# Sparse attention into a routed expert layer: wider token rows, later gathers, an earlier first pair

## The chip, the cores and the metric

The kernel runs on one core of one Trainium2 chip. The metric is device time of one execution in microseconds; lower is better. Matmuls run on TensorE (PE), elementwise work and reductions on VectorE (DVE), copies out of PSUM and exponentials on ScalarE (ACT). GpSimd (POOL) does small copies and issues most DMAs, among them all indirect ones; SyncE (SP) issues the rest.

## The reference

Attention over 4 images x 8 heads of 768 tokens and 64 columns: each query sees the keys nearer than 16 places and, for each block of 32 tokens, one summary (the columnwise maximum of the keys, the mean of the values). The result, 3072 tokens of 512 columns, goes through a layer of 8 experts of which one is used for each token:

```python
k_sum = k.reshape(B, H, nb, block, D).max(axis=3)      # block = 32
v_sum = v.reshape(B, H, nb, block, D).mean(axis=3)
mask_l = np.abs(pos[:, None] - pos[None, :]) < window  # window = 16
a = softmax over [masked q.k/8, q.k_sum/8 + log(block)]
x = a @ concat(v, v_sum)                               # as (3072, 512) rows
logits = x @ w_gate + modality_bias[modality_id]
e_idx = argmax(logits); gate_w = softmax(logits)[e_idx]
out[token] = gate_w * (relu(x @ w1[e_idx]) @ w2[e_idx])
```

The inputs are drawn once; w1 is 8 x 512 x 1024 and w2 8 x 1024 x 512, all in fp32. The kernel computes in fp16 with fp32 sums.

## The kernel before

The work comes in 16 **pairs** of heads (4 images x 4 pairs), numbered `n`. For each pair, `load` has GpSimd fetch keys, values and queries with a cast to fp16 (three DMAs). `keys` transposes keys and values on TensorE (`pk`), ScalarE copies them into `kv`, and GpSimd copies the borders between chunks of 64 tokens. `summaries` reduces the blocks on VectorE (`ks`), and GpSimd spreads them into `kv` (L236). `queries` transposes the queries, `blocks` the values with their summaries. `scores` (in two halves) multiplies, takes the exponential and a band mask, and `values` (two halves) multiplies with the values and writes the normalized rows into `xb`, a tile of one image's token rows. `features` transposes `xb` into `xT`. Each engine runs its instructions in the order in which the program emits them, and that order is written out by hand: the main loop at the end works on pair `n` while it prepares pairs `n+1` and `n+2` and loads `n+5`.

When an image is done, `route(b)` runs. It is a generator that the main loop advances by `tick()` between other work: a `yield` more is one place later in the order, on every engine. It computes the gate's logits (`pl`), the winning expert (`oh`), the rank of each token among those of its expert with matmuls by triangular and all-ones matrices (`pr`), and counts (`pc`). Then GpSimd writes each token's row of `xb` to its place in `xs`, a DRAM buffer sorted by expert, with six indirect DMAs (L381). A row holds 512 fp16 columns, the gate weight and the token's number. `take` (called by `route`) then makes a list of tiles of 256 rows: whole tiles of one expert for the first three images (2, 4 and 2 tiles), all that is left for the last.

`rows` fetches a tile's rows into `xr`. For the first three images one plain DMA from SyncE does, at a row number read from the list. For the last image the list has a row number for each of 256 places (`gi`), and GpSimd gathers with two indirect DMAs (L458). `weights` loads an expert's weights where they differ from those in the buffer. `expert_tile` is a generator too, advanced by `pump()`: `turn` transposes the rows (`px`, copied to `xg`), the first layer (`ph`, L498) is copied with a relu to `hT`, and the second layer (`pmo`, L509) is scaled by ScalarE into `ot` (L514) and written to the output with two indirect DMAs (L515). The transposes of tile `i+1` lie inside tile `i`. `enlist` takes up a list: it calls `rows` for every tile of it, queues them in `todo`, and `ahead` starts as many as there are weight buffers (two).

13 tiles of 256 rows run in this draw: 0 to 7 from the first three images, beside the attention of later pairs; 8 to 12 after the last one. How many of the last are needed is read by every engine into a register (`nt`, L642) before they run, and a ladder of branches follows.

The lines that matter most:

```python
XW = DM + 4                                    # fp16 columns in a row of xs, xb, xr
...
for j in range(lst["T"]):                      # enlist
    rows(lst, j, lst["i0"] + j)
    todo.append((lst, j, lst["i0"] + j))
ahead()
...
early_constants()                              # before the main loop
keys(0)
load(2)
summaries(0)
queries(0)
scores(0, 0)
```

Of the kernel before, what the change touches and what calls it, by code (L numbers as in the profile page):

```python
# [22 lines left out]
def kernel(  # L23
# [12 lines left out]
    nc = tc.nc  # L36
# [10 lines left out]
    P8 = S // C8  # L47
    WK, NB = 96, S // 32
    KR = WK + NB
    XW = DM + 4  # L50
    RP = N + 256
    NROW = 256 + E * RP
    NWB = 2
# [23 lines left out]
    def load(n):  # L77
        b, cc = pairs[n]
        loaded[n] = []
        for name, src in (("kn", k), ("vn", v), ("qn", q)):  # L80
# [5 lines left out]
            loaded[n].append(dst)  # L86


    load(0)
    load(1)  # L90
    pidx = const.tile([128, 1], FP32, name="pidx")
    nc.gpsimd.iota(pidx, pattern=[[0, 1]], base=0, channel_multiplier=1,
                   allow_small_or_imprecise_dtypes=True)
    cidx = const.tile([128, 128], FP32, name="cidx")
    nc.gpsimd.iota(cidx, pattern=[[1, 128]], base=0, channel_multiplier=0,
                   allow_small_or_imprecise_dtypes=True)
    ident = const.tile([128, 128], FP16, name="ident")
    nc.vector.tensor_scalar(ident, cidx, pidx, None, op0=ALU.is_equal)
    for kv, vb in zip(kvs, vbs):
        nc.vector.memset(kv[:, :, 0, 64:80], 0.0)  # L100
        nc.vector.memset(kv[:, :, NT - 1, 80:96], 0.0)
        nc.vector.memset(kv[:, :, :, KR:128], 0.0)
        nc.vector.memset(vb[0:WK, :, :, D:D + 1], 1.0)
        nc.vector.memset(vb[WK:KR, :, :, D:D + 1], 32.0)
    tok = const.tile([128, NJ], I32, name="tok")
    nc.gpsimd.iota(tok, pattern=[[128, NJ]], base=0, channel_multiplier=1)
    midc = const.tile([NJ, 128], mybir.dt.int64, name="midc")
    nc.sync.dma_start(midc, moe_modality_id.rearrange("(j p) -> j p", p=128))
    mb0 = const.tile([128, 2, E], FP32, name="mb0")
    nc.sync.dma_start(mb0, moe_modality_bias.unsqueeze(0).to_broadcast([128, 2, E]))  # L110
    ge = const.tile([128, 4], FP32, name="ge")
    for i, at in enumerate((32.0, 64.0, 80.0)):
        nc.vector.tensor_scalar(ge[:, i:i + 1], pidx, at, None, op0=ALU.is_ge)
# [57 lines left out]
    def later_constants():  # L171
        for t in xrs[-2:]:
            nc.vector.memset(t, 0.0)
        nc.sync.dma_start(xs[0:256].rearrange("(a p) d -> p a d", p=128), xrs[-1].bitcast(I32))
        yield
        nc.gpsimd.dma_start(wg, moe_w_gate.rearrange("(c p) e -> p c e", p=128))
        nc.vector.tensor_scalar(upper, cidx, pidx, None, op0=ALU.is_gt)
        nc.vector.tensor_copy(prow[:, 0:1], pidx)
        nc.vector.tensor_scalar_add(prow[:, 1:2], pidx, 128.0)
        yield  # L180
        nc.vector.tensor_scalar_mul(k256, cidx[:, 0:KM].unsqueeze(2).to_broadcast([128, KM, E]), 256.0)
        nc.vector.tensor_tensor(rowc, k256, erow[:, None, :].to_broadcast([128, KM, E]), op=ALU.add)
        nc.vector.tensor_copy(tab[:, 2], cidx[:, None, 0:E].to_broadcast([128, KM, E]))
        mdiff = work.tile([128, E], FP32, tag="mdiff", bufs=1, name="mdiff")
        nc.vector.tensor_tensor(mdiff, mb0[:, 1, :], mb0[:, 0, :], op=ALU.subtract)
        yield
        mh = work.tile([NJ, 128], FP16, tag="mh", bufs=1, name="mh")
        nc.vector.tensor_copy(mh, midc.bitcast(I32)[:, 0::2])
        yield
        yield  # L190
        pm = bank([128, NJ], FP16, "pm")
        nc.tensor.transpose(pm, mh, ident[0:NJ, 0:NJ])
        yield
        midf = work.tile([128, NJ], FP32, tag="midf", bufs=1, name="midf")
        nc.vector.tensor_copy(midf, pm)
        yield
        nc.vector.tensor_tensor(base, midf.unsqueeze(2).to_broadcast([128, NJ, E]),
                                mdiff[:, None, :].to_broadcast([128, NJ, E]), op=ALU.mult)
        yield
        nc.vector.tensor_tensor(base, base, mb0[:, 0:1, :].to_broadcast([128, NJ, E]), op=ALU.add)  # L200
# [77 lines left out]
    xbs = {}  # L278

    def values(n, half):  # L280
        b, cc = pairs[n]
        s = st[n]
        pT, vb = s.pop(("pT", half)), s["vb"]
        po = bank([128, 2, 3, D + 1], FP32, "po")
        for h in range(2):
            for tl in range(6):
                nc.tensor.matmul(po[64 * (tl % 2):64 * (tl % 2) + 64, h, tl // 2, :],  # L287
                                 pT[0:KR, h, tl, :], vb[0:KR, 6 * half + tl, h, :])
        rec = work.tile([128, 2, 3], FP32, tag="rec", name="rec")
        nc.vector.reciprocal(rec, po[:, :, :, D])  # L290
        if b not in xbs:
            xbs[b] = work.tile([128, NC, XW], FP16, tag="xb", bufs=2, name="xb")
            nc.vector.tensor_copy(xbs[b][:, :, DM:XW].bitcast(I32)[:, :, 1:2],
                                  tok[:, ds(NC * b, NC)].unsqueeze(2))
        xo = xbs[b][:, 3 * half:3 * half + 3, ts(cc, 128)].rearrange("p c (h d) -> p h c d", h=2)
        nc.vector.tensor_tensor(xo, po[:, :, :, 0:D], rec.unsqueeze(3).to_broadcast([128, 2, 3, D]),  # L296
                                op=ALU.mult)
# [26 lines left out]
    def route(b):  # L324
# [23 lines left out]
        ex = small([128, NC, E], tag="ex")  # L348
        nc.scalar.activation(ex, lg, AF.Exp)
        yield  # L350

        pr = bank([128, NC, E], FP32, "pr")
        nc.tensor.matmul(pr, ident, bc(erow, NC), start=True, stop=False, skip_group_check=True)
# [11 lines left out]
        with nc.allow_low_precision(reason="whole numbers: rows, and counts up to 24"):  # L365
            posi = small([128, NC], U32, tag="posi", bufs=2)
            nc.vector.reduce_sum(posi, rk, axis=AX.X)
            xb = xbs.pop(b)
            nc.vector.reciprocal(xb[:, :, DM:DM + 2].bitcast(FP32), se.unsqueeze(2))
            yield  # L370
            if b == 0:
                nc.vector.reduce_sum(tot, oh.rearrange("p c e -> p e c"), axis=AX.X)
            else:
                t2 = small([128, E], FP16, tag="t2")
                nc.vector.reduce_sum(t2, oh.rearrange("p c e -> p e c"), axis=AX.X)
                nc.vector.tensor_tensor(tot, tot, t2, op=ALU.add)
        yield
        pc = bank([128, E], FP32, "pc")
        nc.tensor.matmul(pc, ones, tot)
# [107 lines left out]
    def expert_tile(i):  # L487
# [6 lines left out]
        for f2 in range(NF // 2):  # L494
            ph = bank([128, 2, 256], FP32, "ph")
            for f in range(2):
                for c in range(NCD):
                    nc.tensor.matmul(ph[:, f, :], w1[:, c, ts(2 * f2 + f, 128)], xg[:, c, :],  # L498
                                     start=(c == 0), stop=(c == NCD - 1))
            yield  # L500
            nc.scalar.activation(hT[:, 2 * f2:2 * f2 + 2, :], ph, AF.Relu)  # L501
        if i + 1 in prep and i + 1 not in heads:
            turn(i + 1)
        for s2 in range(2):
# [22 lines left out]
    def enlist(lst):  # L527
        heads.add(lst["i0"])
        for j in range(lst["T"]):
            rows(lst, j, lst["i0"] + j)  # L530
            todo.append((lst, j, lst["i0"] + j))
        ahead()

    def ahead():

        while todo and todo[0][2] < min(ended[0] + NWB, guessed[0]):
            lst, j, i = todo.popleft()
            weights(lst, j, i)
            pending.append(expert_tile(i))

# [10 lines left out]
    def drain(g):  # L551
        for _ in g:
            pass
# [12 lines left out]
    def weights_ahead(n):  # L566

        for p in {1: (0,), 2: (1, 2), 3: (3,), 4: (4,), 5: (5,), 6: (6,), 7: (7,)}.get(n, ()):
# [5 lines left out]
            if p == 7:  # L574
                guessed[0] = NTILE + NWB
                ahead()

    early_constants()
    keys(0)
    load(2)  # L580
    summaries(0)
    queries(0)
    scores(0, 0)
    blocks(0)
    keys(1)
    load(3)
    summaries(1)
    load(4)
    queries(1)
    side.append(later_constants())  # L590
    for n in range(np_):
        b, cc = pairs[n]
        u = [int(c) for c in UNITS.get(n, "000000")]
        scores(n, 1)
        tick()
        if n and cc == 0:
            features(n - 1)
            assert not side
            side.append(route(b - 1))
        pump(u[0])  # L600
        if n + 2 < np_:
            keys(n + 2)
        if n + 5 < np_:
            load(n + 5)
        weights_ahead(n)
        tick()
        pump(u[1])
        values(n, 0)
        tick()
        if n + 2 < np_:  # L610
            summaries(n + 2)
        tick()
        pump(u[2])
        if n + 2 < np_:
            queries(n + 2)
        tick()
        pump(u[3])
        if n + 1 < np_:
            blocks(n + 1)
            tick()  # L620
            scores(n + 1, 0)
        tick()
        pump(u[4])
        if cc:
            features(n - 1)
        tick()
        values(n, 1)
        tick()
        if b and cc == 1:
            tick(99)  # L630
            enlist(lists[b - 1])
        pump(u[5])
# [6 lines left out]
    r = lists[B - 1]  # L639
    i0 = r["i0"]  # L640
    enlist(r)
    nt = nc.values_load(r["li"][0:1, NSURE + 1, 0:1], min_val=NSURE, max_val=FIN)  # L642
    while todo or len(pending) > 1:
        drain(pending.popleft())
        ended[0] += 1
        ahead()
# [38 lines left out]
```

The softmax here doesn't subtract the row's maximum and nothing guards it: scores larger than these inputs give would overflow.

## Time and profile before

| | |
|---|---|
| time, median of 3 | 269.67 us (268.44 to 271.12) |
| span of the profiled execution | 266.6 us |
| TensorE matmul busy | 193.5 us (73%) |
| VectorE busy | 128.1 us (48%) |
| ScalarE busy | 122.4 us (46%) |
| GpSimd busy | 126.3 us (47%) |
| DMA moved | 27.08 MB |

A share of the span is a mean over stages with different limits: the first pair (to about 15 us), pairs alone (to 77 us), pairs with tiles beside them (to 186 us), and the last image's routing and tiles (from there on). The last output write is issued at 256.25 us; its landing and the ladder of branches close the span. What limits a stage has to be read from its own windows and timeline. In a timeline row the columns are the start and duration in us, the engine (PEld is TensorE's weight load), the line, the operation, output and inputs, shapes and count, and in brackets the engine's idle time before it with what ended that.

### The profile page before, as it was taken

The page shows a single profiled execution, that of the slowest core. Times are in us where ns is not written, and L with a number is a line of the kernel's source. Part 1 is how long each engine was busy: PE and PEld are TensorE (multiplying, and loading weights), DVE is VectorE, ACT ScalarE, POOL GpSimd, SP SyncE. Part 2 cuts the span into 40 slices and gives each one's busy share as a digit, 9 for nine tenths or more (in the row PEclk, how much of TensorE's full clock was granted, in tenths as well). Part 3 has the DMA queues.
Part 4 walks back from the last instruction along what each step waited for, and adds up shares of the span by engine and source line. Part 5 has one row for each costly group of instructions (what it writes and reads, how often), then busy time and mean ns, then how long its engine had stood idle before and what let it go on. Part 6 is the DMA issues. An engine that isn't in the chain of part 4 may idle for free. (4 is left out here: it accounts for less than half of the span.)

```text
span 266.6 us, 6691 instructions
## 1 busy us (share of the span) xinstructions
PE 193.5 (73%) x2684; PEld 137.1 (51%) x2684; DVE 128.1 (48%) x361; ACT 122.4 (46%) x211; POOL 126.3 (47%) x198
## 2 busy tenths in 40 slices
PE   0375966753859895597998776998973829999920
PEld 0264844642747663264767534675751603677610
DVE  0859899661975565096456824753770100111000
ACT  1355894422736572173866435562423113454520
POOL 7529797536661347556132174131576751223220
PEclk9999996555558999577999995999999965999995
DMA  6838999993795948268511022421123321122100
GB/s 84 128 61 117 193 165 200 205 200 109 110 225 84 113 64 183 102 87 182 151 39 42 2 81 83 119 82 40 72 94 122 104 88 39 43 79 80 73 19 0
DMA packets 20090, 27.08 MB, mean 102 GB/s; under 512 B 2876, under 2 KB 16468, under 8 KB 20052
## 3 DMA queue, kind: packets, MB, share of 16 engines
q0 software_dynamic: 17424, 24.17, 45.0%
q1 hardware_dynamic: 2628, 2.41, 3.3%
q8 instruction: 23, 0.38, 0.6%
q14 instruction: 15, 0.12, 0.1%
HBM read 85.27 MB, written 10.25 MB: 358 GB/s over the span
## 5 line engine op out<-in xcount | busy, mean ns | idle before, releaser
L509 PE MATMUL pmo<-w2b,hT 128*128 128x512 f16 x208 | 53.4, 407 | 6.1 <-issue 4.2
L498 PE MATMUL ph<-xg,w1b 128*128 128x256 f16 x416 | 54.7, 283 | 3.6 <-issue 3.6
L515 POOL DMA_INDIRECT out_dram<-ot,at x26 | 25.9, 995 | 49.3 <-ACT ot L514 40.7
L498 PEld LDWEIGHTS <-w1b 128*128 128x128 f16 x416 | 39.6, 100 | 12.4 <-issue 4.8
L272 ACT ACTIVATE pT<-pss 128x384 f16<-128x384 f32 x64 | 28.0, 496 | 29.6 <-PE pss L268 29.3
L501 ACT ACTIVATE hT<-ph 128x512 f16<-128x512 f32 x52 | 30.6, 605 | 20.3 <-remote 13.9
L223 ACT COPY kv<-pk 128x768 f16<-128x768 f16 x32 | 24.5, 814 | 32.8 <-PE pk L222 13.5
L509 PEld LDWEIGHTS <-hT 128*128 128x128 f16 x208 | 20.2, 102 | 30.7 <-issue 8.5
L381 POOL DMA_INDIRECT xs<-xb,posi x24 | 24.5, 1022 | 15.8 <-DVE rec L290 8.4
L514 ACT ACTIVATE ot<-pmo,xr 128x512 f32<-128x512 f32 x26 | 18.0, 692 | 28.9 <-PE pmo L509 26.2
L481 DVE COPY xg<-px 128x1024 f16<-128x1024 f16 x13 | 8.9, 684 | 45.0 <-PE px L479 32.9
L273 DVE TENSOR_TENSOR pT<-pT,bmask 96x768 f16<-96x768 f16 x32 | 19.6, 613 | 17.1 <-ACT pT L272 16.2
L226 POOL COPY kv<-kv 128x352 f16<-128x352 f16 x16 | 8.1, 509 | 28.6 <-ACT kv L223 28.4
L290 DVE RECIPROCAL rec<-po 128x6 f32<-128x6 f32 x32 | 6.0, 187 | 30.6 <-PE pq L244 13.2
L255 PE MATMUL pv<-ident,kv 128*128 128x128 f16 x192 | 18.8, 268 | 1.8 <-POOL kv L236 1.0
L287 PE MATMUL po<-vb,pT 120*64 120x65 f16 x384 | 15.3, 215 | 6.5 <-issue 2.9
L244 PE MATMUL pq<-ident,qn 96*64 96x96 f16 x256 | 13.5, 244 | 7.2 <-issue 6.3
L255 PEld LDWEIGHTS <-kv 128*128 128x128 f16 x192 | 15.8, 123 | 5.2 <-issue 2.2
L296 DVE TENSOR_TENSOR xb<-po,rec 128x384 f16<-128x384 f32 x32 | 17.8, 557 | 1.2 <-issue 0.2
L268 PE MATMUL pss<-qT,kv 64*128 64x64 f16 x384 | 13.3, 211 | 5.9 <-POOL kv L236 5.9
L246 ACT COPY qT<-pq 128x768 f16<-128x768 f16 x16 | 13.0, 810 | 9.6 <-PE pq L244 9.5
L256 ACT COPY vb<-pv 120x768 f16<-120x768 f16 x16 | 12.9, 804 | 8.1 <-PE pv L255 8.1
(122 smaller groups left out, 279.6 us busy)
## 6 DMA issues: line engine op xcount, KB each, us to landing
w1b<-in_moe_w_dram POOLq DMA_DIRECT2D x13, 1024.0 KB
w2b<-in_moe_w_dram POOLq DMA_DIRECT2D x13, 1024.0 KB
kn<-in_k_dram POOLq DMA_DIRECT2D x16, 192.0 KB
vn<-in_v_dram POOLq DMA_DIRECT2D x16, 192.0 KB
qn<-in_q_dram POOLq DMA_DIRECT2D x16, 192.0 KB
xr<-xs SPq DMA_DIRECT2D x8, 258.0 KB, 4.0
w1b<-in_moe_w_dram POOLq DMA_DIRECT2D x4, 512.0 KB
w2b<-in_moe_w_dram POOLq DMA_DIRECT2D x4, 512.0 KB
```

What stands on the lines that cost most here:

```text
L223: nc.scalar.copy(kv[:, i, :, 0:64].rearrange("p t (s c) -> p t s c", c=C8), bass.AP(pk.tensor, pk.offset, [pk.ap[0], [8, NT], [1, 8], [P8, ...
L255: nc.tensor.transpose(pv[:, tl, :], kv[:, 1, 6 * half + tl, :], ident)
L272: nc.scalar.activation(pT[:, h], pss[h], AF.Exp, scale=SCALE)
L273: nc.vector.tensor_tensor(pT[0:WK], pT[0:WK], bmask[0:WK, None, 6 * half:6 * half + 6, :].to_broadcast([WK, 2, 6, 64]), op=ALU.mult)
L287: nc.tensor.matmul(po[64 * (tl % 2):64 * (tl % 2) + 64, h, tl // 2, :], pT[0:KR, h, tl, :], vb[0:KR, 6 * half + tl, h, :])
L296: nc.vector.tensor_tensor(xo, po[:, :, :, 0:D], rec.unsqueeze(3).to_broadcast([128, 2, 3, D]), op=ALU.mult)
L381: apart("xs", nc.gpsimd.indirect_dma_start(out=xs[:, :], out_offset=bass.IndirectOffsetOnAxis(ap=posi[:, c:c + 1], axis=0), in_=xb[:, c, : ...
L498: nc.tensor.matmul(ph[:, f, :], w1[:, c, ts(2 * f2 + f, 128)], xg[:, c, :], start=(c == 0), stop=(c == NCD - 1))
L501: nc.scalar.activation(hT[:, 2 * f2:2 * f2 + 2, :], ph, AF.Relu)
L509: nc.tensor.matmul(po, hT[:, f, ts(s2, 128)], w2[:, f, :], start=(f == 0), stop=(f == NF - 1))
L514: nc.scalar.activation(ot, po, AF.Copy, scale=gt)
L515: apart("out", nc.gpsimd.indirect_dma_start(out=out[:, :], out_offset=bass.IndirectOffsetOnAxis(ap=at[:, s2:s2 + 1], axis=0), in_=ot[:], i ...
```

## The change

It has four parts.

- The rows of `xs`, `xb` and `xr` grow from 516 to 544 fp16 columns, that is from 1032 to 1088 bytes, which is 17 x 64. The added columns of `xb` are set to zero. The aim is that each row begins and ends on a boundary of 64 bytes.
- Of the last image's tiles, `enlist` gathers the rows of the first two only; a new function `fetch` gathers a later tile's rows within the tile two before it (or when the tile is started). The aim is that GpSimd, which issues in order, isn't occupied by ten gathers at once. The register load for the branches moves from ahead of these tiles to between them.
- At the start, two index vectors are made ahead of the first loads; the borders of each pair's buffers are set just before that pair instead of all at once, and the early constants come after the first pair's summaries, so that the first scores can start earlier.
- `route` yields three times more (twice ahead of `pr`, once ahead of `pc`), `later_constants` once more, and at the end of an image `keys(n + 2)` goes ahead of `features` and the new route, so that TensorE has other work while VectorE prepares what a routing matmul needs.

The diff, cut to its core:

```diff
-    XW = DM + 4
+    XW = DM + 32
...
-    load(0)
-    load(1)
     pidx = ...iota;  cidx = ...iota
+    load(0)
+    load(1)
     ident = ...
-    for kv, vb in zip(kvs, vbs):
+    def borders(i):
+        kv, vb = kvs[i], vbs[i]
         nc.vector.memset(kv[:, :, 0, 64:80], 0.0)      # and four more
+    borders(0)
...
     # values
             xbs[b] = work.tile([128, NC, XW], FP16, tag="xb", bufs=2, name="xb")
+            nc.vector.memset(xbs[b][:, :, DM:XW], 0.0)
...
     # route
         nc.scalar.activation(ex, lg, AF.Exp)
+        yield
+        yield
         yield
         pr = bank([128, NC, E], FP32, "pr")
...
+        yield
         yield
         pc = bank([128, E], FP32, "pc")
...
     # expert_tile, after the first layer
+        fetch(i + 2)
         if i + 1 in prep and i + 1 not in heads:
...
     # enlist
-            rows(lst, j, lst["i0"] + j)
+            if lst["gi"] is None or j < 2:
+                rows(lst, j, lst["i0"] + j)
...
+    def fetch(i):
+        for lst, j, i2 in todo:
+            if i2 == i and i not in prep:
+                rows(lst, j, i)
...
     # ahead
-            lst, j, i = todo.popleft()
+            lst, j, i = todo[0]
+            fetch(i)
+            todo.popleft()
...
     # before the main loop
-    early_constants()
     keys(0)
-    load(2)
     summaries(0)
+    load(2)
+    borders(1)
+    early_constants()
     queries(0)
...
     # main loop
         scores(n, 1)
         tick()
+        pump(u[0])
+        if n + 2 < np_:
+            keys(n + 2)
         if n and cc == 0:
             features(n - 1)
             side.append(route(b - 1))
-        pump(u[0])
-        if n + 2 < np_:
-            keys(n + 2)
...
     # the last tiles
-    nt = nc.values_load(r["li"][0:1, NSURE + 1, 0:1], ...)
     while todo or len(pending) > 1:
+        if ended[0] == i0 + NSURE - 2:
+            nt = nc.values_load(r["li"][0:1, NSURE + 1, 0:1], ...)
         drain(pending.popleft())
```

More of the change, by code (lines that the diff above doesn't have):

```diff
@@ L107 @@
     midc = const.tile([NJ, 128], mybir.dt.int64, name="midc")
-    nc.sync.dma_start(midc, moe_modality_id.rearrange("(j p) -> j p", p=128))
     mb0 = const.tile([128, 2, E], FP32, name="mb0")
     nc.sync.dma_start(mb0, moe_modality_bias.unsqueeze(0).to_broadcast([128, 2, E]))
+    nc.sync.dma_start(midc, moe_modality_id.rearrange("(j p) -> j p", p=128))
     ge = const.tile([128, 4], FP32, name="ge")
@@ L376, in route @@
                 nc.vector.tensor_tensor(tot, tot, t2, op=ALU.add)
+        yield
         yield
@@ L576, in weights_ahead @@
                 ahead()
+    keys(0)
+    summaries(0)
+    load(2)
+    borders(1)
     early_constants()
-    keys(0)
-    load(2)
-    summaries(0)
     queries(0)
@@ L585 @@
     keys(1)
+    summaries(1)
     load(3)
-    summaries(1)
     load(4)
+    borders(2)
     queries(1)
@@ L641 @@
     enlist(r)
-    nt = nc.values_load(r["li"][0:1, NSURE + 1, 0:1], min_val=NSURE, max_val=FIN)
     while todo or len(pending) > 1:
+        if ended[0] == i0 + NSURE - 2:
+            nt = nc.values_load(r["li"][0:1, NSURE + 1, 0:1], min_val=NSURE, max_val=FIN)
         drain(pending.popleft())
```

## The prediction

> **What bounds the kernel now.** I read the table by windows of 10 us first, then the timeline of three stretches in which it looked weak, then the list of waits. Of the windows (columns: PE, weight load, DVE, ACT, POOL busy, granted clock, DMA share, GB/s) these carry the argument:
>
> ```profile
> 0.00:10.00 10.00, 2.34 (x48) 2.09 (x48) 3.30 (x24) 3.58 (x4) 5.95 (x15) 1.00 0.81 117
> 10.00:20.00 10.00, 4.97 (x102) 4.49 (x104) 6.59 (x24) 3.82 (x7) 3.69 (x7) 1.00 0.43 65
> 30.00:40.00 10.00, 7.34 (x214) 6.19 (x212) 9.89 (x20) 9.42 (x17) 9.35 (x15) 1.00 1.12 167
> ...
> 200.00:210.00 10.00, 5.68 (x38) 2.87 (x37) 0.76 (x2) 2.77 (x5) 6.85 (x9) 1.00 0.38 116
> 210.00:220.00 10.00, 4.10 (x31) 2.55 (x28) 0.19 (x1) 1.25 (x3) 6.09 (x8) 0.77 0.29 92
> 220.00:230.00 10.00, 9.82 (x55) 5.67 (x56) 0.57 (x2) 4.67 (x9) 2.05 (x4) 0.72 0.14 52
> 230.00:240.00 10.00, 10.00 (x70) 6.33 (x68) 1.52 (x4) 4.66 (x8) 2.05 (x4) 1.00 0.15 55
> ```
>
> There is no single bound. In the first 15 us everything waits for the first pair. From 20 to 190 us several engines share the load (DVE 9.9 of 10 us at 30 to 40). At 230 to 250 TensorE is full: the ideal end. At 200 to 220 nothing is full: TensorE has half its work, VectorE none, and only GpSimd is occupied. The timeline of the start shows why the first scores are late:
>
> ```profile
> 6.35 0.85 PE L222 MATMUL pk<-ident,kn 96*64 96x96 f16 x16 [6.35 <-DVE ident L98]
> ...
> 12.43 0.95 DVE L233 TENSOR_REDUCE ks<-kv 128x24 f16<-128x768 f16 x1
> 13.29 0.94 DVE L235 TENSOR_REDUCE ks<-kv 128x24 f16<-128x768 f16 x1
> 14.30 0.67 POOL L236 COPY kv<-ks 128x576 f16<-128x576 f16 x1 [1.97 <-DVE ks L235]
> 15.03 0.50 PE L268 MATMUL pss<-qT,kv 64*128 64x64 f16 x12 [5.92 <-POOL kv L236]
> ```
>
> The keys were copied by 8.74 us, but VectorE had 3 sets of border memsets, the mask and the early constants ahead of `ks`. In the routing of the first image TensorE stands in order behind VectorE twice:
>
> ```profile
> 54.16 0.20 PE L354 MATMUL pr<-oh,upper 128*128 128x48 f16 x1 [2.57 <-DVE oh L347]
> ...
> 57.38 0.17 PE L379 MATMUL pc<-tot,ones 128*128 128x8 f16 x1 [2.00 <-DVE tot L372]
> ```
>
> And the timeline of the tail:
>
> ```profile
> 202.11 1.07 POOL L458 DMA_INDIRECT xr<-xs,gi  x1 [1.44 <-issue]
> ...
> 208.52 3.67 PE L498 MATMUL ph<-xg,w1b 128*128 128x256 f16 x32
> ...
> 215.19 0.60 ACT L501 ACTIVATE hT<-ph 128x512 f16<-128x512 f32 x1 [5.01 <-remote]
> 215.32 1.02 POOL L515 DMA_INDIRECT out_dram<-ot,at  x1 [0.30 <-DMA xr<-xs,gi]
> ...
> 219.81 0.69 DVE L481 COPY xg<-px 128x1024 f16<-128x1024 f16 x1 [12.09 <-remote]
> ...
> 225.91 3.66 PE L498 MATMUL ph<-xg,w1b 128*128 128x256 f16 x32
> ```
>
> Tile 8 (the first of the last image) starts its first layer at 208.52, tile 9 only at 225.91: 17.4 us. The next tiles start 7.39 us apart (233.31, 240.70, 248.09), so 10.0 us are lost here. The ten gathers run from 202.11 to 215.01, and the consumers of tile 8's matmuls (ACT `hT`, DVE `xg`) stay idle until 215 and 219.5, although the matmuls are recorded by 212.2. TensorE is also recorded in small bursts of about five, with gaps put down to "issue", during the six row writes at 57.5 to 65.1, 104.1 to 111.5 and 153 to 161. So something in long rows of indirect DMAs holds TensorE's completions up; the trace doesn't tell what.
>
> **What the Trainium skill says.** "TensorE: Matmul & The Clock Gate", Part 1: the clock falls to half after an idle window and needs a few us of work to return. The trace agrees: granted clock 0.77 and 0.72 at 210 to 230, and 128x512 matmuls then run 0.42 us apart against 0.21; idle TensorE costs twice. "DMA: Bandwidth & Descriptors", Anatomy of one DMA: about 2 us of an HBM write are the wait for its receipt, beyond issue. The trace has 3.2 us: the last row write is issued by 198.10, and the gathers' wait ends at 201.3. The same page, How a descriptor splits into AXI transactions: a start that isn't on 256 B costs extra beats. Rows of 1032 B start badly, rows of 1088 B start on 64 B and still mostly not on 256; four rows took 0.18 us in the trace, and two 2048 B output rows 0.17. I see no DMA engine that is the limit there, and credit the padding by itself with nothing.
>
> **The change part by part.**
>
> *Start.* The two iotas (0.41 us by their starts, 5.58 to about 5.97) now go ahead of the loads, so every load is 0.4 us later: K lands at 5.8, V's transposes end 0.4 later, and the copies of both at 9.15. `ident` no longer gates (the 6.35 wait goes). VectorE has only one set of borders and the mask before `ks` (work of about 4.5 us from about 2.5, so done by 7). V's reduction, 0.94 after 9.15, ends at 10.1; the POOL copy 0.67 ends near 10.9; first scores at about 11.0 against 15.03: 4.0 us earlier. Against it, `load(2)` moves behind that copy, from 10.39 to 10.9, and its last data land near 16.3 instead of 15.8 (DMA ceased at 15.8 by the packets' times), where pair 2's queries would be wanted at 20.97-4.0=17.0, its keys at 15.3: a wait of up to 0.5. `early_constants` (10.79 to 12.5 before) moves behind `ks`, beside ACT's first exponentials. Credit 3.5; bounds 1.5 and 4.5. It lasts, as loads are issued pairs ahead and TensorE never waits for them after 8.3 us.
>
> *Routing with more yields; `keys` ahead of `features`.* TensorE's waits for `pr` and `pc` are 2.57+2.00 in the first image, 1.08 in the second, 1.29+0.45 in the third: 7.4 us. Its waits of `pt` for `xb` (2.39, 0.89, 0.80: 4.1 us) now lie behind the 32 key transposes. To pay: `pl` now follows `pt` with no other TensorE work between, and needs the `xT` copy (0.55 plus some 0.3 of hand-over), 3 x 0.9=2.7. And the lists come three ticks later; a pair of about 9 us has eight ticks, so some 3 us. Queued behind a list are SP's load of `xr` and, behind that, the `px` transposes; that wait was already 3.06 us at 77.8. In the last image one more `ph` group (1.03) precedes `pr`, so the row writes start about 1.1 us later. I credit a net 1.5 for the three images (bounds -4 and +6) and charge 1.1 in the tail.
>
> *Gathers one tile ahead.* At the head of the last list 4 gathers are issued instead of 10: at 1.31 us apart they end at 202.11+4x1.31=207.4 (plus the 1.1), and tile 8's first layer meets none of the other six. Each later tile gets two (2.6 us) beside its two output writes (2x0.98): 4.6 of 7.39 us of POOL, so they fit, and a gather is asked for a whole tile (7.4 us) before its transposes, against some 4.3 from issue to use at 202.11 to 206.36. Behind a gather on POOL now stand the output writes of that tile, each late by at most 2.6 us, and `ot` has three buffers. Of the 10.0 us lost I keep 2.6 for one pair of gathers during tile 8: gain 7.4. The price of a gather to TensorE is not in the trace by itself; bounds: 0 gained if two gathers hold a tile up as ten did, 10 if not at all.
>
> *Register load of `nt` moved* (L642; TensorE idle 1.36 ahead of 197.88, ACT 5.18): credited with nothing, because tile 8 waits for its rows until 206 anyway; it now falls between full tiles, 0.5 us per queue, behind TensorE's queued matmuls.
>
> *Small ones.* Four memsets of `xb`'s tail (about 0.15 each on VectorE), wider `xr` (5% of 2 x 0.49 us), 5% more row bytes: the row writes are issued at 1.29 us each, so bytes hide behind issue. Nothing. The swap of `mb0` and `midc` frees `g1` earlier, hidden.
>
> Sum: -3.5-1.5-(7.4-1.1)=-11.3, so 269.7-11.3=258.4 us.
>
> **Rivals.**
> *A, as worked out:* 258.4. For it: the 10 us gap stands alone in the tail, and the start is a plain chain. Chance 0.58.
> *B, absorbed:* the front's gain meets full DMA queues (share 1.12 to 1.18 at 30 to 60 us) or the later lists, and the held-up TensorE returns with each pair of gathers; only some 4 us stay: 265.7. For it: VectorE is full at 30 to 40, and the clock may fall in the wait before tile 8. Chance 0.20.
> *C, the aligned rows also end the hold-ups:* three trains of row writes take TensorE some 7 to 10 us for work of 3 to 5, so 4 each: 258.4-12=246.4. Against it: the hold-up at 103.4 begins before the first row write lands, behind output writes whose rows are aligned. Chance 0.12.
> *D, slower:* the lists' 3 us are paid in each of three images (+9 less 4 of saved waits), gathers hold up each of four tiles by 2.6 (so no gain of the 10), the last routing +1.1, the start -3.5: about 272.5. For it: `px` already waits 3.06 on `xr`. Chance 0.10.
>
> **How the numbers follow.** The predicted time is A's. Low 247.5 takes in most of C and the upper bounds of A's parts; high 267.5 takes in B. Out of it are D and part of C, under 2 in 10. Faster by over 1% (under 267.0): A, C and 0.13 of B: 0.83. Within 1%: the rest of B and a little of D: 0.08. Slower: 0.09.
>
> **What would show it.** First scores near 11 us; no TensorE wait at `pr` or `pc` over 1 us; the `px` wait on `xr` in the first image no more than 5 us; after the last row writes four gathers in a row, then pairs; tiles 8 and 9 under 11 us apart, tiles 9 to 12 still 7.4. Wrong if tiles 9 to 12 stretch above 8.5 us, if first scores stay after 13 us, or if TensorE isn't held up any more during the row writes (then C).

## The result, and the profile after

The changed kernel is faster: 249.83 us (249.01 to 250.73, 4 runs) against 269.06 us for the kernel before in the same series (265.48 to 271.12, 4 runs), a ratio of 0.936 with a 95% interval of 0.926 to 0.946. Repeated in two later series the ratio was 0.931 (0.924 to 0.938) and 0.982 (0.970 to 0.994). That the two differ so much is the main finding below. Medians take in all runs, but ratios leave out those in a slower, disturbed state, so a difference given "by the ratio" can be smaller than that of two medians: here it is 17 us, not 19.

The same windows as before the change, now of the kernel after (PE, weight load, DVE, ACT, POOL busy, granted clock, DMA share, GB/s):

```profile
0.00:10.00 10.00, 2.55 (x48) 1.99 (x48) 5.34 (x26) 3.31 (x4) 6.14 (x16) 1.00 0.80 112
10.00:20.00 10.00, 7.08 (x168) 6.29 (x168) 8.16 (x36) 8.61 (x15) 7.09 (x13) 1.00 0.75 105
30.00:40.00 10.00, 7.70 (x187) 6.41 (x183) 9.20 (x18) 8.07 (x15) 8.67 (x15) 0.77 1.19 203
190.00:200.00 10.00, 4.62 (x20) 2.15 (x21) 1.47 (x4) 1.29 (x2) 6.55 (x9) 0.66 0.41 136
200.00:210.00 10.00, 10.00 (x82) 7.48 (x80) 0.76 (x2) 5.65 (x9) 5.20 (x7) 1.00 0.24 80
210.00:220.00 10.00, 10.00 (x80) 6.96 (x78) 1.52 (x4) 4.96 (x8) 4.69 (x9) 1.00 0.30 106
220.00:230.00 10.00, 10.00 (x72) 6.52 (x71) 0.76 (x2) 4.63 (x8) 4.77 (x7) 1.00 0.16 58
```

The second window holds 168 matmuls where it held 102: the pairs begin sooner. One weak window is left before the last tiles (190 to 200), where there were two, and a third at 0.72 of the clock; from 200 on TensorE is full at full clock, with GpSimd's gathers beside it (POOL is busy for 5.2 and 4.7 us of each 10, where the last windows of before had 2.05).

The timeline of the start, in which every step is the one the prediction followed:

```profile
5.15 0.85 PE L227 MATMUL pk<-ident,kn 96*64 96x96 f16 x16 [5.15 <-DMA kn<-in_k_dram]
...
6.88 0.95 DVE L238 TENSOR_REDUCE ks<-kv 128x24 f16<-128x768 f16 x1 [2.20 <-ACT kv L228]
...
8.50 0.95 DVE L240 TENSOR_REDUCE ks<-kv 128x24 f16<-128x768 f16 x1 [0.67 <-ACT kv L228]
...
9.51 0.67 POOL L241 COPY kv<-ks 128x576 f16<-128x576 f16 x1
...
10.42 0.50 PE L273 MATMUL pss<-qT,kv 64*128 64x64 f16 x12 [0.89 <-ACT qT L251]
```

Now the keys' transposes wait for the keys, and the reductions for ScalarE's copies: a chain with no foreign work in it. The routing of the first image, TensorE's rows:

```profile
48.31 0.20 PE L362 MATMUL pr<-oh,upper 128*128 128x48 f16 x1 [1.85 <-DVE oh L353]
...
51.30 0.19 PE L388 MATMUL pc<-tot,ones 128*128 128x8 f16 x1
```

The wait at `pr` fell from 2.57 to 1.85, that at `pc` from 2.00 to nothing. And the tail:

```profile
191.98 1.07 POOL L467 DMA_INDIRECT xr<-xs,gi  x1 [0.30 <-issue]
...
196.00 1.01 POOL L467 DMA_INDIRECT xr<-xs,gi  x1 [0.30 <-issue]
...
199.88 3.66 PE L507 MATMUL ph<-xg,w1b 128*128 128x256 f16 x32
...
203.93 1.05 POOL L467 DMA_INDIRECT xr<-xs,gi  x1 [0.87 <-issue]
...
207.28 0.93 PE L507 MATMUL ph<-xg,w1b 128*128 128x256 f16 x7
```

Four gathers, then a pair in each tile; tile 9 follows tile 8 after 7.40 us instead of 17.39.

So the 18.4 us between the profiled spans (266.6 and 248.2) come in three portions, read off the starts of the same instruction in both: 4.6 by the first scores, 10.0 by the last image's logits (`pl`, 186.15 and 176.19), and 18.6 by tile 9's first layer (225.91 and 207.28). The start gave 4.6, pairs and routing 5.4, the tail 8.7.

One more view matters: the list of waits that the profile puts down to "remote", where an engine waited although the matmul it needed was recorded as ended, and no instruction is named as the releaser. (The ends of matmuls are modelled by the profile, not measured.) All are engines waiting for TensorE. The time given is the engine's whole idle time before the instruction, ordinary waiting included: of the 12.1 us of `xg` below only the last 4.4, from 215.4 to 219.8, lie behind the recorded end of the transposes. First the kernel before, then the kernel after (total us, times, longest):

```profile
ACT hT L501 <- remote: 13.9, 3, 5.2
...
DVE xg L481 <- remote: 12.1, 1, 12.1
...
DVE rec L290 <- remote: 8.6, 1, 8.6
...
ACT kv L223 <- remote: 6.4, 2, 4.2
```

```profile
ACT pT L277 <- remote: 10.7, 3, 5.3
...
DVE rec L295 <- remote: 5.7, 1, 5.7
...
DVE xT L314 <- remote: 4.8, 1, 4.8
...
ACT kv L228 <- remote: 2.6, 1, 2.6
...
ACT qT L251 <- remote: 1.6, 1, 1.6
...
ACT hT L510 <- remote: 0.9, 1, 0.9
```

These are the hold-ups of the prediction. They stand beside trains of indirect DMAs in both kernels. Those of the last tiles (`hT`, `xg`, 26.0 us) are all but gone. Those beside row writes are still there: of the second and third image in the kernel before, of all three in the kernel after.

### The profile page after: what moved, and what is told of

Same layout as the page of the kernel before. It is cut to its first block, busy times and chain, and to the rows that moved or that the text cites. A ratio compares the mean times of both kernels' runs of the same rounds, so it can differ in the third digit from the quotient of the medians.

```text
span 248.2 us, 6696 instructions
## 1 busy us (share of the span) xinstructions
PE 188.5 (76%) x2684; PEld 135.6 (55%) x2684; DVE 125.6 (51%) x365; ACT 122.3 (49%) x211; POOL 125.8 (51%) x198
## 3 DMA queue, kind: packets, MB, share of 16 engines
HBM read 85.46 MB, written 10.44 MB: 386 GB/s over the span
## 5 line engine op out<-in xcount | busy, mean ns | idle before, releaser
L507 PE MATMUL ph<-xg,w1b 128*128 128x256 f16 x416 | 53.1, 278 | 2.7 <-issue 2.5
L519 PE MATMUL pmo<-w2b,hT 128*128 128x512 f16 x208 | 52.8, 401 | 2.9 <-ACT hT L510 1.7
L507 PEld LDWEIGHTS <-w1b 128*128 128x128 f16 x416 | 39.1, 99 | 11.0 <-issue 4.2
L524 ACT ACTIVATE ot<-pmo,xr 128x512 f32<-128x512 f32 x26 | 18.0, 691 | 31.3 <-PE pmo L519 18.5
L390 POOL DMA_INDIRECT xs<-xb,posi x24 | 25.4, 1057 | 8.1 <-issue 5.8
L278 DVE TENSOR_TENSOR pT<-pT,bmask 96x768 f16<-96x768 f16 x32 | 18.2, 570 | 13.8 <-ACT pT L277 13.4
L260 PE MATMUL pv<-ident,kv 128*128 128x128 f16 x192 | 17.5, 257 | 4.4 <-issue 2.5
L260 PEld LDWEIGHTS <-kv 128*128 128x128 f16 x192 | 14.8, 117 | 6.7 <-issue 3.2
L488 PE MATMUL px<-ident,xr 128*128 128x128 f16 x104 | 9.8, 247 | 10.8 <-DMA xr<-xs 6.2
L292 PE MATMUL po<-vb,pT 120*64 120x65 f16 x384 | 14.8, 215 | 3.5 <-issue 2.9
L238 DVE TENSOR_REDUCE ks<-kv 128x24 f16<-128x768 f16 x16 | 15.1, 944 | 3.3 <-ACT kv L228 3.3
```

Of the source, the lines that this page charges most:

```text
L238: nc.vector.reduce_max(ks[:, 0], kv[:, 0, :, 0:64].rearrange("p t (g s) -> p t g s", g=2), axis=AX.X)
L260: nc.tensor.transpose(pv[:, tl, :], kv[:, 1, 6 * half + tl, :], ident)
L278: nc.vector.tensor_tensor(pT[0:WK], pT[0:WK], bmask[0:WK, None, 6 * half:6 * half + 6, :].to_broadcast([WK, 2, 6, 64]), op=ALU.mult)
L390: apart("xs", nc.gpsimd.indirect_dma_start(out=xs[:, :], out_offset=bass.IndirectOffsetOnAxis(ap=posi[:, c:c + 1], axis=0), in_=xb[:, c, : ...
L519: nc.tensor.matmul(po, hT[:, f, ts(s2, 128)], w2[:, f, :], start=(f == 0), stop=(f == NF - 1))
L524: nc.scalar.activation(ot, po, AF.Copy, scale=gt)
```

## The experiments

Twelve kernels ran, in four series on four chips; those of one series shared a chip and runs of the kernel before. The chip of the first pair of profiles is not on record, and no chip served in two series, so a difference between chips cannot be told from one between times. "A chip with hold-ups" below means a series in which they were seen. This table has the landmarks of all profiles, one for each kernel: us from the start of the span to the first scores, and to the first layer of tiles 7, 8 and 9. "Remote" says whether the list of waits has any such line.

| kernel | remote | first scores | tile 7 | tile 8 | tile 9 | 7 to 9 | span |
|---|---|---|---|---|---|---|---|
| before | yes | 15.03 | 194.61 | 208.52 | 225.91 | 31.3 | 266.6 |
| after | yes | 10.42 | 184.41 | 199.88 | 207.28 | 22.9 | 248.2 |
| a_gather10 | no | 10.90 | 174.37 | 190.20 | 197.59 | 23.2 | 238.2 |
| a_narrow | no | 11.01 | 173.57 | 189.13 | 196.53 | 23.0 | 237.2 |
| a_oldstart | no | 15.04 | 175.59 | 191.25 | 198.64 | 23.1 | 239.3 |
| a_oldroute | no | 10.65 | 171.51 | 186.56 | 194.87 | 23.4 | 235.5 |
| a_again | yes | 10.44 | 183.38 | 198.98 | 206.38 | 23.0 | 247.1 |
| b_again | yes | 15.01 | 190.72 | 214.24 | 224.53 | 33.8 | 265.3 |
| a_oldkeys | yes | 10.79 | 185.24 | 200.79 | 208.18 | 22.9 | 248.9 |
| a_oldyield | yes | 10.54 | 182.59 | 197.69 | 205.08 | 22.5 | 245.4 |
| a_third | no | 10.81 | 172.21 | 188.04 | 195.43 | 23.2 | 236.4 |
| a_gather10_2 | no | 10.77 | 173.36 | 188.99 | 196.39 | 23.0 | 236.9 |
| a_lasthead | no | 10.17 | 173.83 | 186.63 | 196.82 | 23.0 | 237.7 |
| b_tail | yes | 15.01 | 190.36 | 205.73 | 213.12 | 22.8 | 253.8 |

**First series: the change with one part undone.** The kernel before took 242.72 us here (55 runs, 239.91 to 249.66), not 269. Nothing in this series can therefore be set against the 249.83 of the changed kernel; the four are compared with each other and with 242.72.

*All ten gathers at the head of the list again:*

```diff
-            if lst["gi"] is None or j < 2:
-                rows(lst, j, lst["i0"] + j)
+            rows(lst, j, lst["i0"] + j)
```

> The changed kernel with all ten gathers of the last image at the head of its list again. Theory G (the train of gathers itself holds TensorE up): tiles 8 to 9 lie about 17.4 us apart again, against 7.4, so about 260 us, 10 above the changed kernel. Rival P (the aligned rows are what freed the tail): tiles 8 and 9 stay under 10 us apart and the time stays within 3 us of the changed kernel's 249.8.

Measured: 238.66 us, ratio 0.985 (0.982 to 0.988), tiles 8 and 9 7.4 us apart. Theory G falls here: ten gathers in a row held nothing up.

*The old row width:*

```diff
-    XW = DM + 32
+    XW = DM + 4
```

> The changed kernel with rows of 1032 bytes instead of 1088. Theory G: the padding is worth nothing, 249 to 251 us, and TensorE's completions come late beside the trains of row writes for as long as in the changed kernel. Rival P: the padding is worth the 5 us by which the pairs and the routing gained more than the start, so about 255 us, and the hold-ups beside the row writes grow by 1 to 2 us each.

Measured: 239.88 us, ratio 0.992 (0.988 to 0.995); its profiled span is 1.0 shorter than that of a_gather10 and its median 1.2 longer. No gain by the padding is shown on this chip. One of about 1.5 us (by the ratios) is not excluded, as the two kernels differ in their gathers too.

*The old start:*

```diff
+    load(0); load(1)           # ahead of the index vectors
...
-    borders(0)
+    for i in range(NK): borders(i)
...
-    keys(0); summaries(0); load(2); borders(1); early_constants()
+    early_constants(); keys(0); load(2); summaries(0)
-    keys(1); summaries(1); load(3); load(4); borders(2)
+    keys(1); load(3); summaries(1); load(4)
```

> The changed kernel with the old order of the start: loads before the index vectors, all borders and the early constants before the first keys, load(2) ahead of the first summaries. Theory G: the first scores come near 15.0 again and the 4.6 us last to the end, so about 254.5 us. Rival B (absorbed): what follows has slack behind DMA and the lists, and 0 to 2 us stay, so 250 to 252.

Measured: 243.23 us, ratio 1.001 (0.998 to 1.005), by the ratios 2.4 to 5.2 us above its three neighbours. First scores at 15.04. The start's gain lasts for the most part, and on this chip no other is seen: with everything else of the change in place, the kernel equals the kernel before.

*The old routing* (both the yields and the order of `keys`):

```diff
         nc.scalar.activation(ex, lg, AF.Exp)
-        yield
-        yield
         yield
...
-        yield                  # ahead of pc
         yield
...
+        if n and cc == 0: features(n - 1); side.append(route(b - 1))
         pump(u[0])
         if n + 2 < np_: keys(n + 2)
-        if n and cc == 0: features(n - 1); side.append(route(b - 1))
```

> The changed kernel without the three added yields in route and with features and route ahead of keys again. Theory G (the routing's slack is worth the rest of the gain, 5.4 us by the start of the last image's logits): about 254 to 255 us, with TensorE's waits for pr and pc back (7 us in all). Rival R (my prediction's 1.5 net, less 1.1 in the tail): 250 to 251, and the 5 us come from something else, the earlier start that meets emptier queues or the padding.

Measured: 237.98 us, ratio 0.980 (0.967 to 0.992), the shortest of the four. No gain by the new routing is seen on this chip.

None of the four traces has a wait put down to "remote". That formed theory H: the hold-ups depend on the chip, and most of what the change brings is what it takes out of them.

**Second series: the two kernels again.** Here the kernel before took 265.45 us (7 runs).

> The changed kernel itself once more, beside the kernel before. In the first four experiments the kernel before took 242.7 us, where it had taken 269.1 beside the changed kernel, and its variants came to 0.98 to 1.00 of it. Theory H: how far TensorE is held up beside trains of indirect DMAs differs between chips, and most of the 19 us was the end of hold-ups that a quieter chip does not have; where the kernel before takes about 243 us the changed kernel takes 237 to 240, a ratio of 0.98 to 0.99. Rival G: the parts add up the same everywhere and each experiment undid one; then the ratio is 0.94 again, about 228 us.

> The kernel before once more, for its trace on this chip. Theory H: where it takes about 243 us, tiles 8 and 9 lie 7.4 to 9 us apart though ten gathers run beside them, against 17.4, the first scores come at 15.0 as before, and one at least of the three trains of row writes passes without a gap over 3 us in TensorE's completions. Rival G: 17.4 us between tiles 8 and 9 again, and the 26 us lie elsewhere, in the pairs.

Measured: the changed kernel 248.12 us, ratio 0.931 (0.924 to 0.938); the kernel before in a single run 267.02. The hold-ups are back in both traces, so this series repeats the first pair and doesn't yet tell H from G. In b_again tile 8 itself is late: its `xg` copy waits until 213.49 for transposes that are recorded as ended by 203.24.

```profile
202.18 1.06 PE L479 MATMUL px<-ident,xr 128*128 128x128 f16 x8
...
213.49 0.69 DVE L481 COPY xg<-px 128x1024 f16<-128x1024 f16 x1 [18.95 <-remote]
```

From tile 7 to tile 9 it takes 33.8 us, where the first profile took 31.3 and the changed kernel takes 23.0.

The parts of the routing alone, `keys` and `features` in their old order, and the three yields taken out:

```diff
+        if n and cc == 0: features(n - 1); side.append(route(b - 1))
         pump(u[0])
         if n + 2 < np_: keys(n + 2)
-        if n and cc == 0: features(n - 1); side.append(route(b - 1))
```

> The changed kernel with features and route ahead of keys again, the added yields kept. Without both it took 238.0 us, a ratio of 0.980. Theory K: the order of keys is what costs on such a chip, since the lists come later: ratio about 0.98, and 1 to 2 us below the changed kernel in the same series. Rival Y: the yields cost, and this one equals the changed kernel within 1 us.

```diff
         nc.scalar.activation(ex, lg, AF.Exp)
-        yield
-        yield
         yield
...
-        yield                  # ahead of pc
         yield
```

> The changed kernel without the three added yields in route, keys still ahead of features. Theory K: equals the changed kernel within 1 us. Rival Y: the lists come three ticks earlier, about 1 us in the last image alone, so the ratio is about 0.98 and the time 1 to 2 us below the changed kernel.

Measured: 251.03 us, ratio 0.942 (0.932 to 0.952), and 249.12 us, ratio 0.942 (0.936 to 0.949). Both expectations missed: neither part, undone, makes the kernel faster here; undoing them costs 2.9 and 1.0 us by the medians, about 3 us each by the ratios. The intervals overlap that of the changed kernel, and the profiled spans (248.9 and 245.4 against 247.1) point in different directions, so no size is claimed.

**Third series: no "remote" waits again.** The kernel before took 245.57 us (7 runs).

> The changed kernel a third time, as the base of the next two. Theory H (two kinds of chip): either the trace has waits on TensorE that the profile puts down to 'remote' and the kernel before takes 265 to 269 us, then 248 to 250 us; or it has none and the kernel before takes about 243, then 237 to 240. Rival G: the ratio is 0.93 to 0.94 whatever the kernel before takes.

Measured: 237.85 us, ratio 0.982 (0.970 to 0.994). G falls, and the numbers are those of H: by the ratios the same two kernels are 17 to 18 us apart where the hold-ups are, and about 4 us where they aren't. The kernel before was not profiled in a series without hold-ups; that it has none there is inferred from its time and from the seven profiles of its variants.

> All ten gathers at the head of the last list again, in the changed kernel. Theory H: on a chip with 'remote' waits tiles 8 and 9 are 16 to 19 us apart again and the time is about 258 us, 10 above the changed kernel; on a chip without them under 9 apart and within 1.5 us of the changed kernel. Rival Q (what TensorE needs is only the rows of tiles 8 and 9, and the ten gathers cost nothing on any chip; the 10 us came with the rest of the change): within 1.5 us of the changed kernel on both.

Measured: 238.37 us, 0.5 above the changed kernel by the medians, 1.3 by the ratios, whose intervals overlap. Rival Q expects the same on such a chip; b_tail below decides. Ten us of a_gather10_2 beside ten gathers, and then ten us of the kernel before, of the first pair, beside the same work:

```profile
189.00:199.00 10.00, 10.00 (x81) 7.47 (x80) 0.76 (x2) 5.54 (x9) 7.91 (x10) 1.00 0.36 121
```

```profile
208.00:218.00 10.00, 5.77 (x46) 3.99 (x43) 0.00 (x0) 1.29 (x2) 7.59 (x12) 0.87 0.29 87
```

GpSimd is as busy in one as in the other, and more bytes move in the first; TensorE is full in the first and half idle in the second. The row writes of the third image in one and the same kernel, first a_third, then the kernel after of the first pair, show the same:

```profile
143.60:153.60 10.00, 9.87 (x137) 6.74 (x135) 7.09 (x29) 6.14 (x13) 8.02 (x11) 1.00 0.24 88
```

```profile
148.00:158.00 10.00, 5.62 (x70) 3.61 (x68) 3.02 (x12) 2.68 (x6) 7.53 (x10) 0.85 0.26 97
```

At the closest the gathers and row writes follow each other every 1.28 to 1.31 us on all chips; what differs is TensorE.

*An attempt to improve the last image*: its first transposes after tile 7's second layer instead of in its midst, and no added yields in its route:

```diff
-            if s2 and i + 1 in heads and i + 1 in prep:
+            if s2 and i + 1 in heads and i + 1 in prep and i + 1 != sum(TAKE):
...
-        yield
-        yield
+        if b < B - 1:
+            yield
+            yield
...
-        yield                  # ahead of pc
+        if b < B - 1:
+            yield
```

> The changed kernel with two edits for the last image alone: no added yields in its route, and the transposes of its first tile after the second layer of tile 7 instead of in its midst. Theory: the row writes come about 1 us sooner, and 3.4 us of second layer fill TensorE's wait for the gathered rows, of which about 1 is lost again to the copy of the transposes: 2 to 3 us below the changed kernel in the same series. Rival: the chain from row writes to gathers and the copy sets the time, and the gain is under 1 us.

Measured: 237.83 us against 237.85. Its timeline at tile 8:

```profile
185.22 0.63 PE L490 MATMUL px<-ident,xr 128*128 128x128 f16 x7 [1.07 <-DMA xr<-xs,gi]
...
186.63 6.46 PE L509 MATMUL ph<-xg,w1b 128*128 128x256 f16 x32 [0.78 <-DVE xg L492]
```

and that of a_third:

```profile
184.83 3.38 PE L519 MATMUL pmo<-w2b,hT 128*128 128x512 f16 x8
...
188.04 3.66 PE L507 MATMUL ph<-xg,w1b 128*128 128x256 f16 x32
```

The first layer did start 2.4 us sooner after the transposes (2.7 after their start at 183.92, against 5.1 after 182.94). But it then took 6.46 us for the same 32 matmuls: the granted clock was 0.54 from 186 to 193. In a_third the slow clock (0.53 from 185 to 188) fell on the eight second-layer matmuls instead, while the copy of the transposes ran anyway. The gain of 2.4 was given back as 2.8. The Trainium skill describes this ("TensorE: Matmul & The Clock Gate", Part 1: after an idle window the clock is halved, and some 3.4 us of work are needed to bring it back). The traces agree on the fall and the return, less on the length: the clock is halved for 6.8 us in both, from 185.6 to 192.4 in a_lasthead, of which 5.8 fall on the first layer, and from 181.0 to 187.8 in a_third, of which 3.0 fall on the second. By these two profiles the work that was moved had been paying the warm-up for the first layer behind it.

**Fourth series: the later gathers alone, in the kernel before.**

```diff
-            rows(lst, j, lst["i0"] + j)
+            if lst["gi"] is None or j < 2:
+                rows(lst, j, lst["i0"] + j)
...
+        fetch(i + 2)           # in expert_tile; fetch as in the change
```

> The kernel before with the later gathers alone: four at the head of the last list, then two a tile; rows of 1032 bytes, the old start, the old route. Theory H: on a chip with 'remote' waits tiles 8 and 9 come to 8 to 11 us apart from 17.4 to 18.5, and the ratio to the kernel before is 0.96 to 0.97; on a chip without them they are 8 to 9 apart and the ratio is 1.00 within 0.006, with first scores at 15.0 and no wait put down to 'remote'. Rival P (the aligned rows freed the tail): on a chip with 'remote' waits over 15 apart and a ratio of 0.99 to 1.00.

Measured: 257.54 us against 265.90 (7 runs), on a chip with "remote" waits; the ratio is 0.981 (0.965 to 0.997), a gain of about 5 us (1 to 9). The timeline at tiles 8 and 9:

```profile
203.19 0.69 DVE L481 COPY xg<-px 128x1024 f16<-128x1024 f16 x1 [9.00 <-PE px L479]
...
205.73 3.66 PE L498 MATMUL ph<-xg,w1b 128*128 128x256 f16 x32
...
213.12 1.15 PE L498 MATMUL ph<-xg,w1b 128*128 128x256 f16 x9
```

`xg` follows its transposes at once, tile 9 follows tile 8 after 7.39 us, and from tile 7 to tile 9 it is 22.8 us, as in the changed kernel, with narrow rows and everything else old. Rival P falls: with narrow rows the spread gathers alone free the tail. Against rival Q, that the ten gathers cost nothing on any chip, speak the tiles: from tile 7 to tile 9 it is 8.5 and 11.0 us less than in the two profiles of the kernel before, though these are of other series. How much of it the whole time shows is known only to lie between 1 and 9. The ratio came out higher than the 0.96 to 0.97 expected; its interval reaches down to 0.965. Ten gathers in the changed kernel on a chip with hold-ups were not run. Nor are hold-ups always gone with the gathers spread: a_oldyield has three "remote" waits between 186 and 197, 15.6 us in all, though it too takes 22.5 us from tile 7 to tile 9.

## Why the prediction was right or wrong

The direction and the mechanisms of tail and start held, and 249.8 lies inside the range (247.5 to 267.5); the sum was too small, -11.3 against -19.2 in medians (-18.4 between the profiled spans, -17 by the ratio). That the range was hit is in part luck: most of the gain belongs to hold-ups that only some chips showed, and where there were none the same change brought only about 4 us.

*Start.* Worked out 4.0 and credited 3.5; measured 4.6 at the first scores (10.42 against the 11.0 expected). The step that was off is "K lands at 5.8": the keys' transposes start at 5.15 (before, the keys were there at 5.37), so the index vectors ahead of the loads cost the keys nothing. The 0.5 held back for a later `load(2)` was not due either: it is issued at 10.12, before at 10.39. That the gain lasts was right: 2.4 to 5.2 in a_oldstart.

*Routing and `keys`.* Credited 1.5 net. By the last image's logits the first pair of profiles gained 5.4 more than the start, the second pair 2.5 (7.1 less 4.6). This is the term that was mis-sized by most, and it isn't a fixed amount: on a chip without hold-ups a_oldroute shows it at nothing. What stands against the gain is visible there. The waits that the prediction counted do go: `pr`, `pc` and `pt` together stand at 12.6 us in a_oldroute (5.4+3.1+4.1) and at 4.8 in a_third (3.1, none, 1.7). But the row writes and lists come later, and two other waits grow, `pv` for a copy of GpSimd's and `px` for the list's rows. TensorE's waits in a_oldroute:

```profile
PE pv L260 <- POOL kv L241: 3.6, 2, 2.2
...
PE px L485 <- DMA xr<-xs: 2.7, 1, 2.7
```

and in a_third:

```profile
PE px L488 <- DMA xr<-xs: 11.0, 2, 9.0
...
PE pv L260 <- POOL kv L241: 9.6, 4, 7.0
```

The timeline of a_third shows what stood in the way:

```profile
58.98 0.94 DVE L240 TENSOR_REDUCE ks<-kv 128x24 f16<-128x768 f16 x1
...
61.23 0.98 POOL L390 DMA_INDIRECT xs<-xb,posi  x1 [0.30 <-issue]
...
62.19 0.70 POOL L241 COPY kv<-ks 128x576 f16<-128x576 f16 x1
...
62.94 1.46 PE L260 MATMUL pv<-ident,kv 128*128 128x128 f16 x12 [7.05 <-POOL kv L241]
```

The summaries were ready at 59.9, but their copy stood on GpSimd behind the row writes until 62.2. Six of the seven profiles without hold-ups, all but a_oldroute, have this wait of `pv` in the first image (7.0 to 7.7 us) and one of `px` in the second (9.0 to 9.5). Rival D foresaw the later lists ("the lists' 3 us are paid in each of three images"); in a_third `px` waits 2.0 us in the first image, 9.0 in the second and none in the third, where a_oldroute has 2.7 in the second alone. So the wait came, though in two images and mostly in one, and nothing of it shows in the whole time (ratios 0.982 and 0.980, in two series). The prediction named what is queued behind a list, but not what is queued on GpSimd behind row writes that come three places later. Why the same edits gain 2.5 to 5.4 where hold-ups are is not settled: a held-up TensorE reaches these waits late, so they cost less there (`pv` 1.8, beside 3.3 without a named releaser, and `px` 7.1 in a_again), but that is an argument, not a run.

*Tail.* Credited 7.4 of 10.0, less 1.1: 6.3. Measured 8.7 in the first pair of profiles, 11.1 in the second. The 2.6 kept back for a pair of gathers during tile 8 is the mis-sized term: beside a pair tile 8 takes no longer, and tiles 9 to 12 start 7.39 us apart as before. The charge of 1.1 for the later row writes was about right (tile 8 comes 15.5 us after tile 7 instead of 13.9). One reading of the tail was off: the prediction has TensorE's matmuls recorded by 212.2, but that is the first layer; the transposes that `xg` waits for are recorded until 215.4, so the hold-up of `xg` is 4.4 us, not 7.

*Register load, small ones, padding.* Credited nothing; a_narrow shows no clear gain by the padding where there are no hold-ups, and b_tail needs no wide rows to free the tail where there are. The wide rows alone on a chip with hold-ups were not tried, nor the register load.

*What would show it.* First scores near 11: yes. No wait over 1 us at `pr` or `pc`: `pc` yes, `pr` no (1.85). The first image's `px` wait under 5: yes (3.0). Four gathers, then pairs, under 11 us and 7.4: yes. Rival C's sign, no more hold-ups by the row writes: not fulfilled, though C's time (246.4) lay nearer to the measured one. A's terms were too small; C's reason was wrong, and its nearness is luck.

## What to carry to other kernels

A train of indirect DMAs had two prices here: the wait of what stands behind it in GpSimd's order, seen at the summaries' copy, and on some chips a hold-up of TensorE beside it. Issuing each gather one stage ahead of its use, in twos, brought tiles 8 and 9 back to 7.4 us apart. A `yield` that lets TensorE do other work while VectorE prepares also delays whatever the same generator issues next, so look at what is queued behind those issues on the other engine. And work taken out of the warm-up of TensorE's clock can pass the warm-up on to what follows, as in a_lasthead.

## What the runs showed of the hardware

- Identical kernels differ from series to series far more than from run to run: the kernel before took 269.1, 265.5 and 265.9 us in three series and 242.7 and 245.6 in two, the changed kernel 249.8 and 248.1 against 237.9. The slower series have "remote" waits in all seven of their profiles, the faster ones in none of seven.
- The mean granted clock is lower in the profiles of the slower series (0.84 to 0.87 against 0.86 to 0.89). It did not start the hold-up of the third image's row writes: in the kernel after, TensorE is busy for only 2.1 of the 4 us from 149.6 to 153.6, at full clock, and the clock falls to half after that, from 155.0 to 161.8. All seven slower profiles have such a fall between 149 and 168; in the seven faster ones the clock is full from 138 to 181.
- Of the 11.8 us by which the spans of the kernel after and of a_third, the same kernel, differ, 7.8 lie in a stretch that the change leaves alone. From the third image's logits to the last image's it is 41.6 to 42.6 us in all seven slower profiles, before and after alike, and 34.7 to 36.7 in the seven faster ones; the row writes of the third image lie in this stretch.
- In a hold-up, matmuls are recorded as ended up to 10 us before the engines that wait for them go on (203.2 to 213.5 in b_again). It was seen only where GpSimd had issued indirect DMAs (gathers, row writes or output writes) within the last 3 us. That these cause it is tested for the gathers alone, by b_tail; no run moved the row writes. Whether the cause lies in the chip, in its memory, in what else runs near it or in the recording, and why only waits for TensorE show it, stays open.
- A change can thus be worth 7% on one chip and 2% on another. The spread gathers, undone in the changed kernel on the one, cost 0.5 to 1.3 us, within the noise; alone in the kernel before on another they brought about 5.
